# One change to a linear-attention and MLP kernel: the MLP's second product by Strassen's method

## The chip, the cores and the metric

The kernel runs on one core of one Trainium2 chip. A core has a matrix engine (TensorE, "PE" in the profile, with its weight loads listed as "PEld"), three engines for elementwise work (VectorE "DVE", ScalarE "ACT", GpSimd "POOL"), and a synchronising engine ("SP") that issues nearly all DMA transfers of this kernel. The metric is the device time of one execution in microseconds (us); lower is better. Several executions are timed, and the median is what counts.

## The reference

Two layers with the same weights, on an input x of 2048 tokens by D = 448. Each layer is a linear-attention block and then an MLP block, both with a layer norm in front and a residual add behind:

```
def _A_ref(x, wqkv, wo):          # 16 heads of 28
    q, k, v = split(x @ wqkv)
    pq, pk = phi(q), phi(k)       # phi(t) = (t + 1 if t > 0 else exp(t)) + 1e-6
    kv = einsum("bhsd,bhse->bhde", pk, v);  z = sum of pk over s
    o = (pq @ kv) / (pq . z + 1e-6)
    return o @ wo

def _B_ref(x, w1, b1, w2, b2):    # F = 1792
    h = gelu(x @ w1 + b1)         # tanh approximation
    return h @ w2 + b2

x = x + _A_ref(layernorm(x), ...)
x = x + _B_ref(layernorm(x), ...)     # and both once more
```

All inputs and outputs are float32. The change touches only `h @ w2`: per layer a 2048 x 1792 matrix times a 1792 x 448 matrix.

## The kernel before, in words

**Arithmetic.** Matmuls use a one-pass type, `float32r`, which keeps fewer bits than float32. To get the accuracy back, each float32 operand is split into a high part (a cast to float32r) and a low part (the operand minus its high part), and each product is made of three matmuls: high x high, high x low, low x high. All three accumulate into the same PSUM bank. The masked key-value product (L681) and the transposes are plain float32 and have no split.

**Attention.** Tokens are handled in 16 tiles of 128. A tile is loaded (`ld`), normalised (`a`, `ar`, `n`), transposed through VectorE's 32 x 32 transposes and a trip to DRAM (`tu`, `st`, `sp`; early tiles by TensorE), and split (`xh`, `xl`) into the buffers XH and XL. TensorE then makes keys and queries (`K`, `Q`, helper `proj`, L547 to L552) and accumulates a Gram matrix in four PSUM banks (`G`). After the last tile the key-value matrix is formed (`kv`, L681), masked to its heads and folded with `wo`. In a second pass over the tiles the queries come back from DRAM (`pl`), are divided by their denominators (`pz`, `pd`, `pm`), transposed (`pu`, `ps`, `pp`, `qh`, `ql`) and multiplied with the folded matrix (`o`, `oc`); `oa` adds the residual, and `la`, `ln`, `mu`, `ms`, `mp`, `yh`, `yl` make the normalised, transposed and split input of the MLP. `lb` adds b2 to x ahead of time.

**MLP.** Tokens go in 4 blocks of 512 per layer. For each block and each of NF = 14 chunks of 128 hidden units, `f` makes the first product transposed (hidden units on partitions, 512 tokens along the free axis; 11 matmuls of 512 columns, L891 to L895), `g` applies bias and Gelu on ScalarE, `gh` casts the high part on ScalarE, `gl` subtracts on VectorE, and `y` adds this chunk's share to the second product: for each of the block's 4 token tiles three matmuls of 448 columns (L918 to L920), with the activation as the stationary operand and w2's parts as the moving one. The four sums stay in the four PSUM banks "acc" for the whole block; `ya` adds them to x, and `ys` stores the tile.

The second product's core is

```
pe.matmul(o, gh[:, r], w2h[:, i, s], start=first, stop=False)
pe.matmul(o, gh[:, r], w2l[:, i, s], start=False, stop=False)
pe.matmul(o, gl[:, r], w2h[:, i, s], start=False, stop=last)
```

**Memory and order.** w1 and w2 are staged piece by piece in layer 0 (`bld`, `bhi`, `blo`; pieces 16 to 29 are w2) and stay in SBUF as high and low parts. Intermediate tiles live in rings with a fixed number of buffers (`BUFS`); the next user of a buffer waits until all readers of its last content are done. The MLP's input for a block takes one of two XH/XL buffers. PSUM has eight banks: four "acc", two "h", two "m". The order of all instructions is written out by hand in `ORDER`, one list of tokens per layer; a token is an operation's name, its tile or chunk number, and after a colon an engine or buffer choice (`a`, `d`, `p`: ScalarE, VectorE, GpSimd). A token with ">" belongs to the next layer, one with "<" to the layer before. Each engine, and SP's DMA queue, runs its own instructions strictly in this order, and waits where an operand is not ready; an instruction behind a waiting one waits too.

## Time and profile before

| | us |
|---|---|
| median of 3 runs | 877.58 |
| lowest and highest run | 875.4 and 878.11 |
| profiled execution: span, first to last instruction (the page gives no other time of it) | 875.6 |
| TensorE busy in it | 870.3 |
| VectorE, ScalarE, GpSimd busy | 477.5, 344.2, 208.7 |
| moved by DMA | 93.71 MB |

A row of a group reads: line, engine, operation, tile written <- tiles read, shapes, count, then total busy time and the mean of one in nanoseconds, then how long the engine was idle just before, and what ended that. A row of the timeline reads: start, duration, engine, line, operation, count. Matmuls overlap in the records, so the distance between the starts of two of them is what one costs, not its duration.

### The profile page before, as it was taken

The numbers are of one execution on the slowest core, as the hardware profiler recorded it, in microseconds if no ns is written. First come the engines' busy times: TensorE is split into PE (matmuls) and PEld (weight loads), VectorE is DVE, ScalarE is ACT, GpSimd is POOL, SyncE is SP. The second block draws the span as 40 slices with busy tenths as digits, with TensorE's granted clock in tenths as the row PEclk, the third lists the DMA queues.
The fourth block names the chain that finished last, engine by engine and source line by source line (L and its number), as shares of the span: only waits on it lengthen the run. The fifth ranks groups of instructions, "written<-read, shape, count | busy, mean of one in ns | idle before, by whom it ended". The sixth has DMA issues, their size and how long they took to land.

```text
span 875.6 us, 11616 instructions
## 1 busy us (share of the span) xinstructions
PE 870.3 (99%) x4189; PEld 774.1 (88%) x4189; DVE 477.5 (55%) x974; ACT 344.2 (39%) x610; POOL 208.7 (24%) x247
## 2 busy tenths in 40 slices
PE   9999999999999999999999999999999999999998
PEld 7999998889888888888899999889898888888887
DVE  7887687758543534442379756875735616212112
ACT  6676744323223223322446555341332232223222
POOL 4555552543210020020022325240311110200000
PEclk9999999999999999999999999999999999999999
DMA  7666545543314203220347442363341251021101
GB/s 240 188 179 223 132 137 160 169 149 94 111 57 107 84 17 112 81 75 25 82 149 232 155 117 64 101 203 109 118 107 43 73 130 64 1 73 36 42 1 43
DMA packets 62762, 93.71 MB, mean 107 GB/s; under 512 B 8816, under 2 KB 57968, under 8 KB 62704
## 3 DMA queue, kind: packets, MB, share of 16 engines
q1 hardware_dynamic: 62400, 92.51, 35.1%
q8 instruction: 33, 0.54, 0.3%
q10 hardware_dynamic: 304, 0.46, 0.2%
q14 instruction: 25, 0.20, 0.1%
HBM read 55.65 MB, written 34.08 MB: 102 GB/s over the span
## 4 chain that ended last, share of the span: by engine, by line
PE 90%; issue 3%; DVE 2%; DMA 2%; ACT 1%; POOL 1%; SPq 0%; POOLq 0%; DVEq 0%; ACTq 0%
PE y L919 10%; PE y L918 10%; PE y L920 10%; PE hp L892 9%; PE hp L891 9%; PE hp L893 9%; PE hp L894 3%; PE hp L895 3%; PE psq L547 2%; PE psq L548 2%; PE psq L549 2%; PE op L827 2%; PE op L828 2%; PE op L826 2%; PE psk L547 1%
## 5 line engine op out<-in xcount | busy, mean ns | idle before, releaser
L910 DVE TENSOR_TENSOR gl<-g,gh 128x512 fp32r<-128x512 f32 x112 | 81.3, 729 | 265.1 <-ACT gh L215 265.1
L900 ACT ACTIVATE g<-hp,b1s 128x512 f32<-128x512 f32 x112 | 76.9, 688 | 258.1 <-PE hp L895 236.1
L919 PE MATMUL y<-w2l,gh 128*128 128x448 f32 x448 | 163.7, 365 | 0.0
L918 PE MATMUL y<-w2h,gh 128*128 128x448 f32 x448 | 163.6, 365 | 0.0
L920 PE MATMUL y<-w2h,gl 128*128 128x448 f32 x448 | 163.6, 365 | 0.0
L892 PE MATMUL hp<-XH,w1l 128*128 128x512 f32 x336 | 130.9, 390 | 0.0
L891 PE MATMUL hp<-XH,w1h 128*128 128x512 f32 x336 | 130.8, 389 | 0.0
L893 PE MATMUL hp<-XL,w1h 128*128 128x512 f32 x336 | 130.8, 389 | 0.0
L215 ACT CAST gh<-g 128x512 fp32r<-128x512 f32 x112 | 69.2, 621 | 137.8 <-PE y L919 131.7
L361 POOL TENSOR_TENSOR brs<-bve,mhalf 128x1 f32<-128x1 f32 x64 | 37.3, 586 | 358.7 <-DVE bve L355 325.5
L918 PEld LDWEIGHTS y<-w2h,gh 128*128 128x128 f32 x448 | 84.1, 188 | 7.4
L919 PEld LDWEIGHTS y<-w2l,gh 128*128 128x128 f32 x448 | 84.1, 188 | 7.3
L920 PEld LDWEIGHTS y<-w2h,gl 128*128 128x128 f32 x448 | 84.1, 188 | 6.6
L893 PEld LDWEIGHTS hp<-XL,w1h 128*128 128x128 f32 x336 | 63.1, 188 | 13.2
L891 PEld LDWEIGHTS hp<-XH,w1h 128*128 128x128 f32 x336 | 63.1, 188 | 12.6
L892 PEld LDWEIGHTS hp<-XH,w1l 128*128 128x128 f32 x336 | 63.1, 188 | 12.5
L757 POOL TENSOR_TENSOR pz<-pq,zb 128x448 f32<-128x448 f32 x32 | 37.3, 1170 | 50.0 <-DVE dn L762 37.1
L539 POOL TENSOR_TENSOR xnl<-x,xnh 128x384 fp32r<-128x384 f32 x32 | 32.6, 1017 | 58.4 <-ACT xnh L215 58.3
L351 DVE BATCH_NORM_STATS2 bst<-x 128x6 f32<-128x448 f32 x64 | 39.5, 617 | 7.7 <-DMA x<-in_A_x_dram 4.2
L894 PE MATMUL hp<-XH,w1x 128*128 128x512 f32 x112 | 43.6, 389 | 0.0
L895 PE MATMUL hp<-XL,w1x 128*128 128x512 f32 x112 | 43.6, 389 | 0.0
L855 POOL TENSOR_TENSOR x<-x,b2b 128x448 f32<-128x448 f32 x32 | 39.5, 1246 | 14.9 <-DVE xm L365 14.9
(174 smaller groups left out, 1569.2 us busy)
## 6 DMA issues: line engine op xcount, KB each, us to landing
x<-in_A_x_dram SPq DMA_DIRECT2D x32, 224.0 KB, 3.5
pq_d<-eq SPq DMA_DIRECT2D x32, 224.0 KB, 2.9
pq<-pq_d SPq DMA_DIRECT2D x32, 224.0 KB, 3.4
x<-x_d SPq DMA_DIRECT2D x32, 224.0 KB, 3.3
sq_a<-sq SPq DMA_DIRECT2D x13, 512.0 KB, 3.0
sp<-sq_a SPq DMA_DIRECT2D x52, 128.0 KB, 3.5
sq_q<-sq SPq DMA_DIRECT2D x12, 512.0 KB, 3.6
sp<-sq_q SPq DMA_DIRECT2D x48, 128.0 KB, 3.1
```

Of the source, the lines that this page charges most:

```text
L215: act.copy(out, src)
L351: dve.bn_stats(st, xs)
L891: pe.matmul(o, w1h[:, c, s], x.moving(x.hi, c), start=(c == 0), stop=False)
L892: pe.matmul(o, w1l[:, c, s], x.moving(x.hi, c), start=False, stop=False)
L893: pe.matmul(o, w1h[:, c, s], x.moving(x.lo, c), start=False, stop=False)
L894: pe.matmul(o, w1x[:, s], x.moving(x.hi, 3), start=False, stop=False)
L895: pe.matmul(o, w1x[:, s], x.moving(x.lo, 3), start=False, stop=True)
L900: act.activation(T[l, "g", n], T[l, "hp", n], AF.Gelu_apprx_tanh, bias=b1s[:, n % NF:n % NF + 1])
L910: dve.tensor_sub(lo, T[l, "g", n], f(hi))
L918: pe.matmul(o, gh[:, r], w2h[:, i, s], start=first, stop=False)
L919: pe.matmul(o, gh[:, r], w2l[:, i, s], start=False, stop=False)
L920: pe.matmul(o, gl[:, r], w2h[:, i, s], start=False, stop=last)
```

## The change

w2 is no longer kept in SBUF. Per block of 512 tokens, the Gelu output is seen as a 2 x 2 matrix of quadrants: token halves of 256 by hidden halves of KC = 7 chunks. w2 is a 2 x 2 matrix too: hidden halves by column halves of HD = 224. Strassen's method in Winograd's form makes the 2 x 2 product from seven products of quadrants or sums of them (P1 to P7), instead of eight.

- **Weights, once, in layer 0** (`vd`, `va`, `vh`, `vl`, `vs`): for each of 7 pairs of chunks both rows of w2 are loaded, the seven weight operands (w2's quadrants and three sums) are made, split into high and low parts, and stored in a DRAM tensor `w2_d`.
- **Reloads** (`cw`): each product of each block reads its 128 x 3136 floats (high and low side by side) from `w2_d` into one of three buffers "Y": 7 x 4 x 2 = 56 reloads, on SP's queue.
- **Activations**: `g` now writes a whole block's Gelu output into a store (the second XH and XL buffers and a new tile `g6`); the MLP's input keeps one XH/XL buffer per layer. `cs` makes the four activation sums on GpSimd, in place where it can, in four pieces each; `ch` and `cl` split each product's operand (four pieces, in rings A/B or E/F), on ScalarE and VectorE.
- **Products** (`cp`): for each piece, chunk and token tile, one matmul of 448 columns (high activation against high and low weights side by side) and one of 224 columns (low activation against high weights, into the right half of the bank). Each product uses two "acc" banks.
- **Results**: `ca` (ScalarE) and `cf` (VectorE) take the two halves of a bank out of PSUM, into a temporary tile or straight onto x; `cx` (GpSimd) adds the temporaries to x's quadrants.
- Gone are `gh`, `gl`, `y`, `u`, `ya` and the w2 pieces of `bld`, `bhi`, `blo`. Everything else does the same work, and both lists of `ORDER` are rewritten throughout.

The diff, with the lists cut to a few lines:

```diff
--- before.py
+++ after.py
 ORDER = (
     (
-        "ld0 a0 ar0 ld1 a1 n0 hot16 wkld0 wkld1:a wkld2 wkld3:a wkh1 wkl1 ht0 wkh0 ar1 wkl0 n1 d0 ht1 hx0 hl0 "
...
+        "ld0 hot16 fl a0 ar0 ld1 a1 ar1 wkld0 wkld1:a tab0 tab1 >tab0 n0 ht0 n1 wkld2 wqld0 wkld3 wqld1 ld3 wkh0 "
...
+        "cs61 ca48 cl102 cs62 >ar4 cs63 cf48 cl104 cp102 ch105:aEF cl105 >st1 cw26 cp103 cf50 "
...
     ),
 )
@@ -140,6 +169,8 @@
     G = 112
     NG = D // G
     TL = D - 64
+    HD = D // 2
+    KC = NF // 2
     LAYERS = 2
 
     consts = ctx.enter_context(tc.tile_pool(name="consts", bufs=1))
@@ -149,7 +180,7 @@
     psum = ctx.enter_context(tc.tile_pool(name="psum", bufs=1, space=bass.MemoryType.PSUM))
     ctx.enter_context(tc.manual_schedule())
 
-    BUFS = {"H": 9, "S": 5, "e": 3, "xn": 2, "A": 2, "B": 2, "E": 2, "F": 2, "X": 2, "tail": 2, "small": 2}
+    BUFS = {"H": 9, "S": 5, "e": 3, "xn": 2, "A": 2, "B": 2, "E": 2, "F": 2, "X": 2, "tail": 2, "small": 2, "Y": 3}
     BANKS = {"acc": 4, "h": 2, "m": 2}
 
     def dram(shape, dt, name):
@@ -168,6 +199,7 @@
         return smalls.tile([128, n], F32, name=name, tag=name, bufs=BUFS["small"])
 
     pq_d = [dram([S, D], F32, f"pq_d{l}") for l in range(LAYERS)]
+    w2_d = dram([7, 128, KC * D], F32, "w2_d")
     x_d = [x0] + [dram([S, D], F32, f"x_d{l}") for l in range(1, LAYERS)] + [y_out]
 
     ones = consts.tile([128, 128], F32R, name="ones")
@@ -195,8 +227,7 @@
     w1h = wts.tile([128, 3, F], F32R, name="w1h")
     w1l = wts.tile([128, 3, F], F32R, name="w1l")
     w1x = wts.tile([128, F], F32R, name="w1x")
-    w2h = wts.tile([128, NF, D], F32R, name="w2h")
-    w2l = wts.tile([128, NF, D], F32R, name="w2l")
+    g6 = wts.tile([128, 6, 512], F32, name="g6")
 
     def rows(t):
         return slice(t * 128, (t + 1) * 128)
@@ -311,18 +342,12 @@
     def bld(l, n, e):
         tag = e or "xn"
         s = T[l, "bg", n] = ring(tag, 512 if tag == "xn" else D, "stg")[:, :D]
-        if n < 16:
-            load_piece(w1[:, n // 4 * D:(n // 4 + 1) * D], n % 4, s, sp)
-        else:
-            sp.dma_start(s, w2[rows(n - 16), :])
+        load_piece(w1[:, n // 4 * D:(n // 4 + 1) * D], n % 4, s, sp)
 
     @op
     def bhi(l, n, e):
         s = T[l, "bg", n]
         eng = ENG[e or "a"]
-        if n >= 16:
-            copy(eng, w2h[:, n - 16], s)
-            return
         sl, c = slice(n // 4 * D, (n // 4 + 1) * D), n % 4
         if c < 3:
             copy(eng, w1h[:, c, sl], s)
@@ -335,14 +360,48 @@
     def blo(l, n, e):
         s = T[l, "bg", n]
         eng = ENG[e or "p"]
-        if n >= 16:
-            eng.tensor_tensor(w2l[:, n - 16], s, f(w2h[:, n - 16]), op=OP.subtract)
-            return
         sl, c = slice(n // 4 * D, (n // 4 + 1) * D), n % 4
         if c < 3:
             eng.tensor_tensor(w1l[:, c, sl], s, f(w1h[:, c, sl]), op=OP.subtract)
         else:
             eng.tensor_tensor(w1x[64:128, sl], s[64:128], f(T[l, "bt", n][64:128]), op=OP.subtract)
+
+    P1, P7, P6, P5, P2, P3, P4 = range(7)
+
+    @op
+    def vd(l, i, e):
+        T["w2o", l, i] = o = ring("Y", KC * D, "w2o").rearrange("p (k h n) -> p k h n", k=7, h=2)
+        sp.dma_start(o[:, P1:P5 + 1:P5 - P1, 1], w2[rows(i), :].rearrange("p (h n) -> p h n", h=2))
+        sp.dma_start(o[:, P2:P3 + 1, 1], w2[rows(KC + i), :].rearrange("p (h n) -> p h n", h=2))
+
+    @op
+    def va(l, i, e):
+        o = T["w2o", l, i][:, :, 1]
+        eng = ENG[e or "p"]
+        eng.tensor_tensor(o[:, P7], o[:, P3], o[:, P5], op=OP.subtract)
+        eng.tensor_tensor(o[:, P5], o[:, P5], o[:, P1], op=OP.subtract)
+        eng.tensor_tensor(o[:, P6], o[:, P3], o[:, P5], op=OP.subtract)
+        eng.tensor_tensor(o[:, P4], o[:, P2], o[:, P6], op=OP.subtract)
+
+    @op
+    def vh(l, i, e):
+        hi, lo = (T["w2o", l, i][:, :, h] for h in range(2))
+        copy(ENG[e or "a"], hi.bitcast(F32R), lo)
+
+    @op
+    def vl(l, i, e):
+        hi, lo = (T["w2o", l, i][:, :, h] for h in range(2))
+        (ENG[e or "p"]).tensor_tensor(lo.bitcast(F32R), lo, hi, op=OP.subtract)
+
+    @op
+    def vs(l, i, e):
+        sp.dma_start(w2_d[:, :, i * D:(i + 1) * D].rearrange("k p n -> p k n"),
+                     T["w2o", l, i].rearrange("p k h n -> p k (h n)"))
 
@@ -365,9 +424,9 @@
         dve.tensor_scalar(out, xs, mv[:, 0:1], rs, op0=OP.subtract, op1=OP.mult)
 
     class Block:
-        def __init__(self):
-            self.hi = ring("XH", 2048, "XH", F32R)
-            self.lo = ring("XL", 2048, "XL", F32R)
+        def __init__(self, r):
+            self.hi = ring(f"XH{r}", 2048, "XH", F32R)
+            self.lo = ring(f"XL{r}", 2048, "XL", F32R)
 
         def pieces(self, t):
             s = slice(t * 512, (t + 1) * 512)
@@ -379,11 +438,10 @@
         def still(self, x, t, c):
             return x[:, (t * 4 + c) * 128:(t * 4 + c + 1) * 128]
 
-    BUFS["XH"] = BUFS["XL"] = 2
-
-    def block(*key):
+    def block(kind, l, b):
+        key = (kind, l, b) if kind == "a" else (kind, l)
         if ("blk", key) not in T:
-            T["blk", key] = Block()
+            T["blk", key] = Block(b % 2)
         return T["blk", key]
 
@@ -894,47 +952,124 @@
         pe.matmul(o, w1x[:, s], x.moving(x.hi, 3), start=False, stop=False)
         pe.matmul(o, w1x[:, s], x.moving(x.lo, 3), start=False, stop=True)
 
+    def gstore(l):
+        if (l, "G2") not in T:
+            T[l, "G2"] = [ring(t, 2048, "g2").rearrange("p (c n) -> p c n", c=4) for t in ("XH1", "XL1")]
+        return T[l, "G2"]
+
+    def gview(l, half, c, k=1):
+        return gstore(l)[half][:, c:c + k] if c < 4 else g6[:, half * 3 + c - 4:half * 3 + c - 4 + k]
+
     @op
     def g(l, n, e):
-        T[l, "g", n] = ring("e", 512, "g")
-        act.activation(T[l, "g", n], T[l, "hp", n], AF.Gelu_apprx_tanh, bias=b1s[:, n % NF:n % NF + 1])
-
-    @op
-    def gh(l, n, e):
-        T[l, "gs", n] = ring("A", 512, "gh", F32R), ring("B", 512, "gl", F32R)
-        copy(ENG[e or "a"], T[l, "gs", n][0], T[l, "g", n])
-
-    @op
-    def gl(l, n, e):
-        hi, lo = T[l, "gs", n]
-        dve.tensor_sub(lo, T[l, "g", n], f(hi))
-
-    def y_mm(l, n, j, s=slice(0, D), o=None):
-        gh, gl = T[l, "gs", n]
         i = n % NF
-        first, last = i == 0, i == NF - 1
-        r = rows(j)
-        o = T[l, "y", n // NF, j][:, s] if o is None else o
-        pe.matmul(o, gh[:, r], w2h[:, i, s], start=first, stop=False)
-        pe.matmul(o, gh[:, r], w2l[:, i, s], start=False, stop=False)
-        pe.matmul(o, gl[:, r], w2h[:, i, s], start=False, stop=last)
-
-    @op
-    def y(l, n, e):
-        for j in range(4):
-            u(l, n * 4 + j, e)
-
-    @op
-    def u(l, n, e):
-        n, j = divmod(n, 4)
-        if n % NF == 0:
-            T[l, "y", n // NF, j] = bank("acc", f"y{j}")[:, :D]
-        y_mm(l, n, j)
-
-    @op
-    def ya(l, t, e):
-        xs = T["x", l, t]
-        dve.tensor_tensor(xs, T[l, "y", t // 4, t % 4], xs, op=OP.add)
+        act.activation(gview(l, i // KC, i % KC)[:, 0], T[l, "hp", n], AF.Gelu_apprx_tanh, bias=b1s[:, i:i + 1])
+
+    def quad(l, r, c, q):
+        return gview(l, c, q * 2, min(2, KC - q * 2))[:, :, r * 256:(r + 1) * 256]
+
+    def sums(l, n):
+
+        bk, q = divmod(n, 4)
+        k = bk % 7
+        if k == P7:
+            return T[l, "s3", bk // 7 * 4 + q]
+        return quad(l, *{P1: (0, 0), P6: (0, 0), P5: (1, 0), P2: (0, 1), P3: (0, 1), P4: (1, 1)}[k], q)
+
+    @op
+    def cs(l, n, e):
+        (b, s), q = divmod(n // 4, 4), n % 4
+        a11, a12, a21, a22 = quad(l, 0, 0, q), quad(l, 0, 1, q), quad(l, 1, 0, q), quad(l, 1, 1, q)
+        eng = ENG[e or "p"]
+        if s == 0:
+            w = a11.shape[1]
+            T[l, "s3", b * 4 + q] = ring("e", 512, "s3")[:, :w * 256].rearrange("p (c n) -> p c n", c=w)
+        out, x, y, o = ((T[l, "s3", b * 4 + q] if s == 0 else None, a11, a21, OP.subtract),
+                        (a21, a21, a22, OP.add), (a11, a21, a11, OP.subtract), (a12, a12, a11, OP.subtract))[s]
+        eng.tensor_tensor(out, x, y, op=o)
+
+    @op
+    def ch(l, n, e):
+        x = sums(l, n)
+        w = x.shape[1]
+        T[l, "chl", n] = [ring(t, 512, nm, F32R)[:, :w * 256].rearrange("p (c n) -> p c n", c=w)
+                          for t, nm in zip(e[1:] or "AB", ("ch", "cl"))]
+        copy(ENG[e[:1] or "a"], T[l, "chl", n][0], x)
+
+    @op
+    def cl(l, n, e):
+        hi, lo = T[l, "chl", n]
+        ENG[e or "d"].tensor_tensor(lo, sums(l, n), f(hi), op=OP.subtract)
+
+    @op
+    def cw(l, n, e):
+        T[l, "w2", n] = ring("Y", KC * D, "w2s", F32R).rearrange("p (c n) -> p c n", c=KC)
+        ENG[e or "s"].dma_start(f(T[l, "w2", n].rearrange("p c n -> p (c n)")), w2_d[n % 7])
+
+    @op
+    def cp(l, n, e):
+        bk, q = divmod(n, 4)
+        hi, lo = T[l, "chl", n]
+        w = T[l, "w2", bk]
+        if q == 0:
+            T[l, "cp", bk] = [bank("acc", f"cp{j}")[:, :D] for j in range(2)]
+        for c in range(hi.shape[1]):
+            i = q * 2 + c
+            for j in range(2):
+                o = T[l, "cp", bk][j]
+                pe.matmul(o, hi[:, c, rows(j)], w[:, i], start=(i == 0), stop=False)
+                pe.matmul(o[:, HD:], lo[:, c, rows(j)], w[:, i, :HD], start=False, stop=(i == KC - 1))
+
+    @op
+    def ca(l, n, e):
+        bk, j = divmod(n, 2)
+        key = (l, "ctt", bk)
+        if key not in T:
+            tag = "e" if bk // 7 == 3 else "W6" if bk % 7 == P7 else "W5"
+            T[key] = ring(tag, 512 if tag == "e" else D, "ct")[:, :D]
+        T[l, "ct", n] = T[key][:, j * HD:(j + 1) * HD]
+        copy(ENG[e or "a"], T[l, "ct", n], T[l, "cp", bk][j][:, :HD])
+
+    @op
+    def cf(l, n, e):
+
+        bk, j = divmod(n, 2)
+        b, k = divmod(bk, 7)
+        o = T[l, "cp", bk][j]
+        if k in (P2, P3, P4):
+            r, c = {P2: (0, 0), P3: (0, 1), P4: (1, 0)}[k]
+            xs = T["x", l, 4 * b + 2 * r + j][:, c * HD:(c + 1) * HD]
+            dve.tensor_tensor(xs, o[:, :HD], xs, op=OP.add)
+            dve.tensor_tensor(xs, o[:, HD:], xs, op=OP.add)
+            return
+        if k == P6:
+            t = T[l, "ct", n] = T[l, "ct", (b * 7 + P1) * 2 + j]
+            dve.tensor_tensor(t, o[:, :HD], t, op=OP.add)
+        t = T[l, "ct", n]
+        dve.tensor_tensor(t, o[:, HD:], t, op=OP.add)
+
+    @op
+    def cx(l, n, e):
+
+        (bk, j), eng = divmod(n, 2), ENG[e or "p"]
+        b, k = divmod(bk, 7)
+        t = T[l, "ct", n]
+
+        def add(r, c, v):
+            xs = T["x", l, 4 * b + 2 * r + j][:, c * HD:(c + 1) * HD]
+            eng.tensor_tensor(xs, xs, v, op=OP.add)
+
+        if k == P1:
+            add(0, 0, t)
+        elif k == P6:
+            s = T[l, "ct", (b * 7 + P7) * 2 + j]
+            eng.tensor_tensor(s, s, t, op=OP.add)
+            add(0, 1, t)
+            add(1, 0, s)
+            add(1, 1, s)
+        else:
+            add(0, 1, t)
+            add(1, 1, t)
 
     @op
     def ys(l, t, e):
```

More of the change, by code (lines that the diff above doesn't have):

```diff
@@ L902, in gh @@
-    @op
-    def gh(l, n, e):
-        T[l, "gs", n] = ring("A", 512, "gh", F32R), ring("B", 512, "gl", F32R)
-        copy(ENG[e or "a"], T[l, "gs", n][0], T[l, "g", n])
-    @op
-    def gl(l, n, e):
-        hi, lo = T[l, "gs", n]
-        dve.tensor_sub(lo, T[l, "g", n], f(hi))
-    def y_mm(l, n, j, s=slice(0, D), o=None):
-        gh, gl = T[l, "gs", n]
-        i = n % NF
-        first, last = i == 0, i == NF - 1
-        r = rows(j)
-        o = T[l, "y", n // NF, j][:, s] if o is None else o
-        pe.matmul(o, gh[:, r], w2h[:, i, s], start=first, stop=False)
-        pe.matmul(o, gh[:, r], w2l[:, i, s], start=False, stop=False)
-        pe.matmul(o, gl[:, r], w2h[:, i, s], start=False, stop=last)
@@ L922, in y @@
-    @op
-    def y(l, n, e):
-        for j in range(4):
-            u(l, n * 4 + j, e)
-    @op
-    def u(l, n, e):
-        n, j = divmod(n, 4)
-        if n % NF == 0:
-            T[l, "y", n // NF, j] = bank("acc", f"y{j}")[:, :D]
-        y_mm(l, n, j)
-    @op
-    def ya(l, t, e):
-        xs = T["x", l, t]
-        dve.tensor_tensor(xs, T[l, "y", t // 4, t % 4], xs, op=OP.add)
+        i = n % NF
+        act.activation(gview(l, i // KC, i % KC)[:, 0], T[l, "hp", n], AF.Gelu_apprx_tanh, bias=b1s[:, i:i + 1])
```

215 rows, old and new, of the table ORDER are left out of this document.

## The prediction

> **What bounds the kernel now.** I read the page first: busy times, then the chain of waits.
>
> ```profile
> span 875.6 us, 11616 instructions
> PE 870.3 (99%) x4189; PEld 774.1 (88%) x4189; DVE 477.5 (55%) x974; ACT 344.2 (39%) x610; POOL 208.7 (24%) x247
> ...
> q1 hardware_dynamic: 62400, 92.51, 35.1%
> ...
> PE 90%; issue 3%; DVE 2%; DMA 2%; ACT 1%; POOL 1%; SPq 0%; POOLq 0%; DVEq 0%; ACTq 0%
> ```
>
> TensorE is busy from end to end (at full granted clock, 1.00 in the stage rows below) and carries 90% of the chain that sets the end; every other engine is at 55% or less. So time is won only by giving TensorE less work, and lost wherever it must wait. What it works on is in the costliest groups:
>
> ```profile
> L919 PE MATMUL y<-w2l,gh 128*128 128x448 f32 x448 | 163.7, 365 | 0.0
> L918 PE MATMUL y<-w2h,gh 128*128 128x448 f32 x448 | 163.6, 365 | 0.0
> L920 PE MATMUL y<-w2h,gl 128*128 128x448 f32 x448 | 163.6, 365 | 0.0
> ...
> L918 PEld LDWEIGHTS y<-w2h,gh 128*128 128x128 f32 x448 | 84.1, 188 | 7.4
> ```
>
> The 365 ns are not a price: matmuls overlap in these records. The price is the distance between starts, so I read TensorE's timeline in the MLP of the first layer: 20 matmuls of the second product in a row, then the same line of the first product two groups later.
>
> ```profile
> 399.69 0.36 PE L919 MATMUL y<-w2l,gh 128*128 128x448 f32 x1
> ...
> 403.54 0.36 PE L920 MATMUL y<-w2h,gl 128*128 128x448 f32 x1
> ...
> 406.26 0.39 PE L891 MATMUL hp<-XH,w1h 128*128 128x512 f32 x1
> ...
> 411.25 0.39 PE L891 MATMUL hp<-XH,w1h 128*128 128x512 f32 x1
> ```
>
> A 448-column matmul costs 3.85 us / 19 = 202.6 ns; a 512-column one 4.99 / 22 = 226.8 ns. The second product is now 3 x 448 = 1344 matmuls of 448 columns: 272.3 us, 31% of the span. Only this part shrinks.
>
> **What TensorE does instead.** Per 512 tokens there are 7 products; each has 7 chunks x 2 token tiles, and for each of these one matmul of 448 columns (high part of the activation against both parts of the weight) and one of 224 (low part against the high part only). With 8 groups of 512 tokens that is 784 pairs: 784 x 202.6 ns = 158.8 us for the wide ones, and 784 narrow ones whose price x decides all. Break-even is x = (272.3 - 158.8) / 784 = 144.7 ns.
>
> No row shows a one-pass matmul of 224 columns. The nearest: the line through the two prices above has a slope of 24.2 ns / 64 columns = 0.378 ns, and gives 202.6 - 224 x 0.378 = 118 ns. But each matmul brings its own weight load, and a narrow one may not hide it. Loads under short matmuls are seen in the masked key-value product, 112 columns each:
>
> ```profile
> 109.75 3.33 PEld L681 LDWEIGHTS kvp<-gt,wvt 128*112 128x112 f32 x32
> 109.95 3.31 PE L681 MATMUL kvp<-gt,wvt 128*112 128x112 f32 x32
> 113.03 0.45 PE L547 MATMUL psq<-wq,XH 128*128 128x448 f32 x1
> ...
> 113.00 0.19 PEld L547 LDWEIGHTS psq<-wq,XH 128*128 128x128 f32 x1
> 113.11 0.19 PEld L548 LDWEIGHTS psq<-wq,XH 128*128 128x128 f32 x1
> ```
>
> 32 loads and matmuls run from 109.95 to 113.03: 96.3 ns each, although one load's record is about 180 ns. So loads are pipelined; scaled from 112 to 128 weights that is 110 ns, and the two loads that follow (128 weights, this kernel's one-pass type) also start 110 ns apart. A load therefore allows 110 ns and the line asks 118; I take 114, between. The ends for the range are two rows that would hold if this reading is wrong: 202.6 ns, the closest that one-pass matmuls ever follow each other in the long runs, and 2 x 96.3 x 224 / 112 = 385 ns, if a narrow matmul ran as the plain f32 product of L681 does (16 products of 112 columns per layer appear as 32 records). A pure 224 x 0.378 = 85 ns I exclude below: it lies under every distance of two such loads.
>
> At 114 ns: 784 x (202.6 + 114) = 248.2 us, **24.1 us less** than 272.3; at 110, 27.2 less; at 118, 21.0 less.
>
> The Trainium skill speaks against the narrow half: "TensorE: Matmul & The Clock Gate", section "LDWEIGHTS (loading the stationary operand)", puts a load at columns / 1.2 ns, an estimate of 107 ns for 128, longer than 224 columns take to stream; the narrow matmul would be bound by its load. With 107 ns the sum would be 30 us less, without the overhead that the rows show.
>
> **What the other engines get.** Prices from rows grouped by shape:
>
> ```profile
> L910 DVE TENSOR_TENSOR gl<-g,gh 128x512 fp32r<-128x512 f32 x112 | 81.3, 729 | 265.1 <-ACT gh L215 265.1
> ...
> L481 DVE TENSOR_TENSOR XL<-tp,XH 128x256 fp32r<-128x256 f32 x4 | 1.6, 421 | 1.0 <-ACT XH L215 1.0
> ...
> L215 ACT CAST gh<-g 128x512 fp32r<-128x512 f32 x112 | 69.2, 621 | 137.8 <-PE y L919 131.7
> ...
> L539 POOL TENSOR_TENSOR xnl<-x,xnh 128x384 fp32r<-128x384 f32 x32 | 32.6, 1017 | 58.4 <-ACT xnh L215 58.3
> ...
> L540 POOL TENSOR_TENSOR xnh<-x,xnh 128x64 fp32r<-128x64 f32 x32 | 12.0, 376 | 0.0
> ```
>
> Per 512 tokens. ScalarE: 14 casts of 512 go (8.7 us); 21 of 512 and 7 of 256, at no more than 0.621 each, come (17.4), with 6 half-width copies out of PSUM (under 3.7). VectorE: 14 subtractions of 512 and 4 adds of 448 go (12.8; the line through the 512 and 256 rows gives 0.65 for 448); 21 of 512 and 7 of 256 (18.3) and 22 adds of 224 columns (0.38 each by the same line, 8.4) come, 26.7. GpSimd: 2.0 ns a column by its two rows, so 12 sums of 512 at 1.27, 4 of 256 at 0.76 and 14 half-width adds at 0.70: 28.1 us new. This all lies beside TensorE's 14 first-product groups (154 x 226.8 = 34.9 us) and 98 pairs (31.0): 66.0 us a block, before 68.9. How full is that cover? The busy time by stage:
>
> ```profile
> 170.00:230.00 60.00, 60.00 (x283) 52.87 (x282) 37.54 (x75) 19.53 (x35) 18.32 (x16) 1.00 0.37 112
> 230.00:300.00 70.00, 70.00 (x333) 62.21 (x332) 34.20 (x66) 18.43 (x30) 7.72 (x8) 1.00 0.28 80
> ```
>
> (columns: TensorE, loads, VectorE, ScalarE, GpSimd busy, clock, share of the DMA engines, GB/s). Scaled to a block of 68.9 us, VectorE has 43.1 in the first stage: minus 12.8, plus 26.7: 57 of 66. GpSimd: 21.0 + 28.1 = 49 of 66. In the second stage VectorE comes to 48. So the extra work is hidden, most tightly in the first block of layer 0, where VectorE is 87% full; past that each microsecond is TensorE's. The preparation of the weight sums (14 stagings go, 7 come, their low parts on VectorE) lies in layer 0's attention, where the page's first slices have VectorE at 7 to 8 tenths; I cost it at nothing, and some 20 us of VectorE work lands there.
>
> **The reloads.** 56 reloads of 128 x 3136 x 4 bytes, 1.606 MB each, on SP's queue, into 3 slots; 90 MB beside today's 93.7. The queue row gives 92.51 MB in 35.1% of 875.6 us: 301 GB/s while the engines are busy.
>
> ```profile
> sq_a<-sq SPq DMA_DIRECT2D x13, 512.0 KB, 3.0
> ```
>
> From the 512 KB row, 1568 KB take 3.0 + 1.08 MB / 301 GB/s = 6.6 us at best and 3.06 x 3.0 = 9.2 at worst. A reload can start when the product three earlier is done. At the tightest, at the end of layer 1, only two products lie between, 2 x 14 x 316.6 ns = 8.9 us; where first-product groups lie between, each adds 2.5 us, and pricing the new list along TensorE leaves 10.8 or more nearly everywhere. So 6.6 is hidden; at 9.2 three reloads are late by 0.3 each, 0.9 us, and I charge that. Behind a waiting reload stand, on SP, the loads and stores that carry the next block's transposes; each may be up to 5.3 us (1.606 MB / 301) later than now.
>
> **Start and end.** At the start the list puts table changes before the first weight cast, and that cast now comes second:
>
> ```profile
> 2.44 1.28 ACT L215 ACT_TABLE_LOAD   x1 [2.44 <-issue]
> ...
> 6.97 0.57 ACT L215 CAST wk<-stg 128x448 fp32r<-128x448 f32 x1 [2.05 <-DMA stg<-in_A_wqkv_dram]
> ```
>
> The load fits into the 2.05 us that ScalarE waits there for a DMA; one cast of 0.57 moves behind it: +0.6. At the end four adds and a store follow the last matmul now, four half-width adds and a store later: nothing.
>
> **Sum:** -24.1 + 0.9 + 0.6 = -22.6. On the profiled execution's span of 875.6 that is 853.0; the median of the runs is 2.0 above that span (877.58), so 855.0.
>
> **Rivals.**
> *The narrow matmul is not cheap* (slower). Place: the 784 narrow matmuls. If the load's 188 ns were time that it holds the array, x is 202.6: 784 x 405.2 = 317.7, +45.4, 923 us; if it runs as L681 does, x = 385, 460.7, +188.4, 1066 us. It decides from 144.7 ns on. For it: no one-pass matmul in the long runs follows another in under 202.6 ns, and none under 448 columns exists in this trace. Against it: L681's loads, recorded as long, every 96 ns. The Trainium skill's "Perfetto Trace Analysis", section "Identifying the Most-Contended Engine", judges TensorE's headroom by load busy time. By the rows that is 88% here, and 224 more loads of 188 ns would make it (4189 + 224) x 188 = 830 us of 855; taken as a bound it would eat all the gain. Chance 0.12.
>
> *Half the gain is lost to waits.* First-product inputs are now one buffer per layer instead of two: the next block's inputs are written only after the last first-product group of this block, and they come through SP's queue behind reloads. Six such hand-overs, 2 us each, and the 87% VectorE stage: 12 us, 867 us. For it: the DMA share rises from 0.28 to about 0.85 in that stage (7 x 5.3 = 37 of 66 us added). Against it: the list leaves second-product work between. Chance 0.15.
>
> *The same waits at full price:* six hand-overs each late by the 5.3 us of a reload ahead, 32 us, 887 us. Chance 0.07.
>
> **How the numbers follow.** Forecast 855 (0.66; its own range 850 to 861: x from 110 to 118, waits from 0 to 5 us). To leave out no more than 2 in 10, I reach from 848 to 885: outside lie the narrow-matmul rival (0.12), about half of the full-price one and a little below. A measurement of this kernel tells about 0.3% (2.6 us) from no change. Faster: forecast and most of the half-lost case, 0.78; same 0.05, from the edges of both wait cases; slower 0.17.
>
> **What would show it.** In the changed profile: starts of wide and narrow second-product matmuls alternate at 203 and 114 ns; were the narrow distance over 145, the forecast falls whatever else happens. TensorE's idle time before the second product's groups should name no DMA of the weight sums for more than 1 us in all, and the reloads should land in 6 to 9 us. VectorE should rise to some 610 us (477.5 + 8 x 13.9 + 20), ScalarE to 443 at most (344.2 + 8 x 12.4), GpSimd to about 430 (208.7 + 8 x 28.1). A gap of several microseconds at the start of a block's first product would show the hand-over; gaps inside the products that end with VectorE would show that its cover is gone.

## The result, and the profile after

The changed kernel takes 914.98 us (median of 4 runs, 912.85 to 917.23) against 877.37 beside it: a ratio of 1.043, 95% interval 1.0409 to 1.0451. It is 4.3% slower; the forecast of 855 and its range up to 885 are both missed, and the change goes the other way.

The page of the changed kernel: span, busy times, the main DMA queue, the chain of waits by engine, the costliest groups of the second product, and the reloads.

```profile
span 912.8 us, 13007 instructions
PE 867.5 (95%) x4413; PEld 757.9 (83%) x4413; DVE 675.9 (74%) x1253; ACT 414.3 (45%) x767; POOL 475.9 (52%) x485
...
q1 hardware_dynamic: 78800, 193.89, 64.3%
...
PE 54%; DVE 20%; POOL 10%; issue 8%; ACT 3%; DMA 2%; SPq 0%; DVEq 0%; POOLq 0%; ACTq 0%
...
L1020 PE MATMUL cp<-w2s,ch 128*128 128x448 f32 x784 | 255.5, 376 | 1.7 <-DVE ct L1049 1.2
L1002 DVE TENSOR_TENSOR cl<-g,ch 128x512 fp32r<-128x512 f32 (+1 forms) x192 | 161.7, 863 | 98.7 <-ACT ch L246 87.3
L1021 PE MATMUL cp<-w2s,cl 128*128 128x224 f32 x784 | 213.6, 272 | 22.1 <-DVE cl L1002 21.7
...
w2s<-w_d SPq DMA_DIRECT2D x56, 1568.0 KB, 7.3
```

Before, TensorE carried 90% of the chain; now it carries 54%, and VectorE and GpSimd 30% between them. So the kernel is no longer bound by TensorE all the way, although TensorE is still listed as 95% busy (its records overlap and fill small gaps).

Did TensorE's work shrink? The timeline of a run of pairs without waits:

```profile
214.04 0.37 PE L1020 MATMUL cp<-w2s,ch 128*128 128x448 f32 x1
214.25 0.26 PE L1021 MATMUL cp<-w2s,cl 128*128 128x224 f32 x1
214.35 0.38 PE L1020 MATMUL cp<-w2s,ch 128*128 128x448 f32 x1
...
216.86 0.38 PE L1020 MATMUL cp<-w2s,ch 128*128 128x448 f32 x1
```

From 214.04 to 216.86 are 9 pairs: 313 ns each (predicted 316.6). 784 pairs cost 245.6 us instead of 272.3: **26.7 us less**, as hoped. With nothing else changed the span would be 875.6 - 26.7 = 848.9. It is 912.8, so 63.9 us of new loss have to be found. The waits of TensorE, by what ended them:

```profile
PE cp L1021 <- DVE cl L1002: 21.7, 30, 1.9
PE hp L951 <- DVE XL L490: 6.8, 5, 2.3
```

and who is behind it on the other engines:

```profile
ACT ch L246 <- PE cp L1020: 143.7, 85, 5.5
...
ACT ch L246 <- POOL g L989: 36.9, 23, 6.9
PEld cp L1021 <- DVE cl L1002: 34.6, 44, 2.1
```

TensorE waits for VectorE's low parts: of the second product (`cl`) and of the first product's input (`XL`). No wait of TensorE names a reload, and these land in 7.3 us, inside the 6.6 to 9.2 of the prediction. The listed idle time is less than 63.9. One reason is that the record of the matmul ahead of a wait lasts longer (0.38 us at 214.35) than the distance to the next start (0.21 at 214.04) and covers the beginning of the wait.

The stretches of the first block of layer 0, in windows of 10 us (columns as in the prediction):

```profile
180.00:190.00 10.00, 9.53 (x50) 8.15 (x49) 7.88 (x12) 4.57 (x10) 6.41 (x6) 1.00 0.92 279
...
212.00:222.00 10.00, 6.90 (x40) 5.64 (x38) 9.93 (x11) 4.50 (x9) 8.86 (x8) 1.00 0.90 322
222.00:232.00 10.00, 9.93 (x45) 8.25 (x46) 8.73 (x21) 2.46 (x4) 3.53 (x4) 1.00 0.69 266
```

Where TensorE is at 6.90 of 10, VectorE is at 9.93 and GpSimd at 8.86. But look at the counts: VectorE is full with 11 instructions in 10 us, and nearly as full with 21. Its instructions have become longer. By shape (VectorE's and GpSimd's groups):

```profile
L1002 DVE TENSOR_TENSOR cl<-g,ch 128x512 fp32r<-128x512 f32 x144 | 130.1, 918 | 71.3 <-ACT ch L246 60.1 <-PE cp L1021 10.8
L490 DVE TENSOR_TENSOR XL<-sp,XH 128x512 fp32r<-128x512 f32 x50 | 49.6, 1007 | 4.1 <-ACT XH L246 2.0 <-DMA x<-x_d 2.0
...
L1049 DVE TENSOR_TENSOR ct<-cp,ct 128x224 f32<-128x224 f32 x64 | 23.9, 381 | 9.6 <-ACT ct L246 9.0
```

The subtraction `cl` of 512 columns takes 918 ns, where the same operation (`gl`) took 729 before, and XL 1007 where it took 749. The add of 224 columns that reads PSUM (L1049) takes 381 ns, the 0.38 of the prediction. What do the long ones have in common? The timeline of three places, both engines together (the last also with TensorE):

```profile
358.92 1.31 POOL L989 TENSOR_TENSOR g<-g,g 128x512 f32<-128x512 f32 x1 [0.62 <-ACT g L966]
359.38 1.40 DVE L1002 TENSOR_TENSOR cl<-s,ch 128x512 fp32r<-128x512 f32 x1 [0.68 <-ACT ch L246]
...
739.26 1.93 POOL L1060 TENSOR_TENSOR x<-x,ct 128x224 f32<-128x224 f32 x2
739.51 3.30 DVE L490 TENSOR_TENSOR XL<-sp,XH 128x512 fp32r<-128x512 f32 x3
740.85 0.40 PE L950 MATMUL hp<-XH,w1l 128*128 128x512 f32 x1
742.86 0.50 PE L951 MATMUL hp<-XL,w1h 128*128 128x512 f32 x1 [1.61 <-DVE XL L490]
...
886.47 0.68 DVE L1002 TENSOR_TENSOR cl<-g,ch 128x512 fp32r<-128x512 f32 x1
887.95 0.67 POOL L1066 TENSOR_TENSOR ct<-ct 128x224 f32<-128x224 f32 x1 [1.99 <-DVE ct L1049]
...
891.57 3.44 POOL L989 TENSOR_TENSOR g<-g,g 128x512 f32<-128x512 f32 x2
892.24 0.39 DVE L1049 TENSOR_TENSOR ct<-cp,ct 128x224 f32<-128x224 f32 x1
```

Alone, a `cl` of 512 takes 0.68 (886.47) and a GpSimd add of 224 takes 0.67 (887.95). At 359.38 a `cl` starts while a GpSimd sum runs that began at 358.92 and ends at 360.23. The `cl` ends at 360.78, 0.55 us after the sum: it does its work only once GpSimd's instruction is over. At 739.51 three XL take 3.30 us instead of 3 x 0.68 = 2.04, beside GpSimd adds, and TensorE loses 1.61 us waiting for them. At 892.24 an add that reads PSUM runs inside a GpSimd sum in 0.39 us, undisturbed. So the reading is: **an elementwise instruction of VectorE with both inputs in SBUF, and a GpSimd instruction on SBUF, exclude each other for the whole length of one instruction.**

The whole trace bears this out. Of the 168 `cl` of 512 columns, the 61 that meet no GpSimd instruction take 645 to 694 ns; the 107 that meet one take up to 1777. In 68 cases a GpSimd sum or add is running when the `cl` starts; in 67 of them the `cl` ends 0.545 to 0.578 us after that instruction, whether it has 224, 256 or 512 columns, and in the last one 0.547 us after the add that follows directly. GpSimd pays as well: an add of 224 takes 0.665 us (median) where it meets no `cl` or XL, and 1.11 where it starts during one. "Both inputs in SBUF" is not the whole rule: the normalising TENSOR_SCALAR of L424, which reads one tile and two values per row, takes 423 to 514 ns where it meets no GpSimd instruction and up to 1481 where it does. The transposes of L460 do not change (567 and 569 ns).

The Trainium skill's "SBUF — State Buffer", section "SBUF: two separate sides", says that the two engines share a port pair that is locked for a whole instruction; the 0.55 us after the sum's end agree. The prediction had not weighed it.

### The profile page after: what moved, and what is told of

The parts are those of the page before. It is cut to its first block, busy times and chain, and to the rows that moved or that the text cites. A ratio compares the mean times of both kernels' runs of the same rounds, so it can differ in the third digit from the quotient of the medians.

```text
span 912.8 us, 13007 instructions
## 1 busy us (share of the span) xinstructions
PE 867.5 (95%) x4413; PEld 757.9 (83%) x4413; DVE 675.9 (74%) x1253; ACT 414.3 (45%) x767; POOL 475.9 (52%) x485
## 4 chain that ended last, share of the span: by engine, by line
PE 54%; DVE 20%; POOL 10%; issue 8%; ACT 3%; DMA 2%; SPq 0%; DVEq 0%; POOLq 0%; ACTq 0%
PE cp L1020 9%; DVE cl L1002 6%; PE hp L951 6%; PE hp L949 6%; PE hp L950 6%; PE cp L1021 5%; POOL g L989 3%; DVE XL L490 2%; PE hp L952 2%; PE hp L953 2%; POOL x L1060 2%; DVE pq L828 1%; PE op L886 1%; PE psq L605 1%; PE psq L606 1%
## 5 line engine op out<-in xcount | busy, mean ns | idle before, releaser
L1020 PE MATMUL cp<-w2s,ch 128*128 128x448 f32 x784 | 255.5, 376 | 1.7 <-DVE ct L1049 1.2
L1002 DVE TENSOR_TENSOR cl<-g,ch 128x512 fp32r<-128x512 f32 (+1 forms) x192 | 161.7, 863 | 98.7 <-ACT ch L246 87.3
L1021 PE MATMUL cp<-w2s,cl 128*128 128x224 f32 x784 | 213.6, 272 | 22.1 <-DVE cl L1002 21.7
L246 ACT CAST ch<-g 128x512 fp32r<-128x512 f32 (+1 forms) x192 | 106.5, 566 | 168.6 <-PE cp L1020 116.0
L1021 PEld LDWEIGHTS cp<-w2s,cl 128*128 128x128 f32 x784 | 150.4, 192 | 38.0 <-DVE cl L1002 34.6
L1020 PEld LDWEIGHTS cp<-w2s,ch 128*128 128x128 f32 x784 | 148.2, 189 | 15.0 <-issue 1.5
L1060 POOL TENSOR_TENSOR x<-x,ct 128x224 f32<-128x224 f32 x96 | 84.0, 898 | 41.2 <-DVE ct L1049 41.2
L989 POOL TENSOR_TENSOR g<-g 128x512 f32<-128x512 f32 (+1 forms) x64 | 78.4, 1230 | 21.9 <-ACT g L966 18.7
L989 POOL TENSOR_TENSOR g<-g,g 128x512 f32<-128x512 f32 x32 | 45.4, 1424 | 30.7 <-ACT g L966 27.8
L490 DVE TENSOR_TENSOR XL<-sp,XH 128x512 fp32r<-128x512 f32 x50 | 49.6, 1007 | 4.1 <-ACT XH L246 2.0
```

What stands on the lines that cost most here:

```text
L246: act.copy(out, src)
L490: dve.tensor_sub(squares(lo), spread_tile(kind, l, t), f(squares(hi)))
L989: eng.tensor_tensor(out, x, y, op=o)
L1002: ENG[e or "d"].tensor_tensor(lo, sums(l, n), f(hi), op=OP.subtract)
L1020: pe.matmul(o, hi[:, c, rows(j)], w[:, i], start=(i == 0), stop=False)
L1021: pe.matmul(o[:, HD:], lo[:, c, rows(j)], w[:, i, :HD], start=False, stop=(i == KC - 1))
```

## The experiments

The theory (A, later A1) is this exclusion. Against it stand: VectorE simply having too much work (B); the reloads, by their traffic or by coming late (C); GpSimd's results merely coming late (A2); and too few buffers between ScalarE, VectorE and TensorE (D). Each run is compared with the kernel before on the same chip, and with the changed kernel's 914.98.

**Sums out of the way.** All of GpSimd's new sums and adds touch one column, and the product P7 reads a plain quadrant instead of its sum, so their real work is left out.

```
-        eng.tensor_tensor(out, x, y, op=o)                   # cs
+        out, x, y = (v[:, :1, :1] for v in (out, x, y))
+        eng.tensor_tensor(out, x, y, op=o)
-            eng.tensor_tensor(xs, xs, v, op=OP.add)          # cx, and s likewise
+            eng.tensor_tensor(xs[:, :1], xs[:, :1], v[:, :1], op=OP.add)
```

> Changes: every GpSimd sum of activations and every GpSimd add of a temporary onto x works on 1 column instead of 224 to 512 (the rest of these sums is left out, and the P7 product reads the plain quadrant); instructions, waits, TensorE work and reloads stay. Theory A (VectorE instructions with two SBUF operands stand still while a GpSimd instruction runs): the 512-column subtraction of the low part falls from 918 ns mean to about 700, VectorE from 676 us by about 60 to 90, and TensorE's waits from 72 us to under 25, so 855 to 870 us. Theory B (VectorE is simply too full, contention is minor): the subtraction stays above 850 ns and the time above 900 us. Theory C (reloads on SP's queue delay the inputs): time above 895 us, the wait of the first product on its input stays.

872.23 us, ratio 0.994 (0.992 to 0.996): 42.7 us of the 63.9 go away with the sums. That is 2 us above the range that A gave; B and C (above 900 and 895) are out as the whole story. VectorE's busy time falls from 675.9 to 603.8 us although not one of its instructions was removed; the prediction's figure for it was 610. That shows what the sums cost, not yet how.

**Reloads cut to a seventh.** Only the first of seven chunks is loaded, and all matmuls of a product use it.

```
-        ENG[e or "s"].dma_start(f(T[l, "w2", n].rearrange("p c n -> p (c n)")), w2_d[n % 7])
+        ENG[e or "s"].dma_start(f(T[l, "w2", n][:, 0]), w2_d[n % 7][:, :D])
```

> Changes: each reload brings only the first of 7 chunks and all matmuls of a product use that chunk (wrong weights, same matmuls, same waits); reload traffic falls from 90 to 13 MB. Theory A: nothing much, 908 to 915 us. Theory B: the same. Theory C: the time falls by more than 20 us, to under 893, and the first product's wait on its input goes.

915.63 us, 1.0435 (1.0414 to 1.0456): the same as the changed kernel, with 13 MB of reloads instead of 90. The reloads and their traffic cost nothing that can be measured.

**The new work on VectorE.** If the two engines only disturb each other, the short VectorE form of the same sums should do better. First the adds `cx` alone, then sums and adds.

```
-        (bk, j), eng = divmod(n, 2), ENG[e or "p"]           # cx
+        (bk, j), eng = divmod(n, 2), dve
-        eng = ENG[e or "p"]                                  # cs, in the second kernel only
+        eng = dve
```

> Changes: only the adds of temporaries onto x (112 half-width adds) move from GpSimd to VectorE; result unchanged. Theory A: VectorE gets 40 us and loses part of its standing still, GpSimd falls by 100 us to 375; time 895 to 912 us. Theory B: VectorE to 716 us or more, time above 920 us. Theory C: close to 915 us.

> Changes: the activation sums and the adds of temporaries onto x move from GpSimd to VectorE, in the same places of the list; result unchanged. GpSimd falls by about 250 us to 215. Theory A: VectorE gets 15 us of work a block (120 us in all) but loses its standing still (about 100 us), so it stays near 690 to 720 us; the 512-column subtraction falls to about 720 ns; time between 875 and 905 us. Theory B: VectorE goes to 790 us, time above 930 us. Theory C: no statement but a time close to 915 us.

925.92 us (1.0557, 1.0539 to 1.0574) and 925.73 (1.0553, 1.0536 to 1.0569): some 11 us slower than the changed kernel, where a gain was expected. Both expectations are missed in their times, although VectorE's busy time in the second (710.6 us) came out as A gave it. The groups, waits and 10 us windows of the second kernel show why:

```profile
L1002 DVE TENSOR_TENSOR cl<-g,ch 128x512 fp32r<-128x512 f32 x144 | 104.1, 735 | 56.1 <-ACT ch L246 46.9 <-PE cp L1021 8.6
...
PE cp L1021 <- DVE cl L1002: 30.1, 30, 2.3
...
190.00:200.00 10.00, 8.47 (x46) 7.49 (x45) 9.79 (x19) 3.94 (x8) 1.59 (x3) 1.00 0.56 189
...
210.00:220.00 10.00, 7.20 (x42) 6.02 (x42) 9.86 (x23) 3.67 (x8) 1.15 (x1) 1.00 0.85 271
```

`cl` is down to 735 ns, so the exclusion is mostly gone; but VectorE stands at 9.8 of 10 all the same, now with 19 and 23 instructions in 10 us, and TensorE waits longer for `cl`. In the products VectorE has no room for this work: per block TensorE needs 98 x 0.313 = 30.7 us for them, and VectorE 21 x 0.68 + 7 x 0.42 = 17.2 for `cl` and 22 x 0.38 = 8.4 for adds out of PSUM; the sums (12 x 0.68 + 4 x 0.42 = 9.8) and the adds (14 x 0.38 = 5.3) make it 40.7. So by this sum there are two limits, not one: shared with GpSimd the exclusion, alone the work itself. The instructions also kept the places that the list had given them for GpSimd, so on VectorE they now stand in line ahead of some `cl`; a list laid out anew was not run, and how much of the 11 us is due to that stays open.

**Is it the exclusion or the lateness?** On top of the one-column kernel, GpSimd is kept busy again: by powers of one column, which touch next to nothing of SBUF, or by adds of 128 x 128; two behind each sum, one behind each add.

```
+    def filler(n):
+        for _ in range(n):
+            pool.tensor_tensor(scrap[:, :1], tiny, mhalf, op=OP.pow)    # first kernel
+            pool.tensor_tensor(scrap, ident, f(ones), op=OP.add)        # second kernel
```

> Changes: the 1-column sums of run e1, and behind each of them GpSimd work of about the old length (two powers of one column, 0.55 us each, behind a sum of activations; one behind an add onto x) that moves almost no data. GpSimd is as busy and as late as in the changed kernel, but hardly touches SBUF. Theory A1 (what costs is that GpSimd and VectorE exclude each other on SBUF): 512-column subtraction 690 to 780 ns, time 868 to 885 us, near e1's 872. Theory A2 (what costs is that GpSimd is late with the sums, and the splits wait for it): 905 to 920 us, with the subtraction below 780 ns.

> Changes: as e5, but the GpSimd work behind each 1-column sum adds two 128 x 128 SBUF tiles into a third (about 0.5 us each) that no other instruction uses. GpSimd is about as busy, and now it reads and writes SBUF. Theory A1: the 512-column subtraction rises to 850 to 950 ns although nothing waits for these adds, time 895 to 920 us, at least 20 us above e5. Theory A2: like e5.

885.07 us (1.0096, 1.0067 to 1.0125) and 883.57 (1.0079, 1.005 to 1.0108). Both add 11 to 13 us to 872.23. The powers show what lateness alone costs, 12.8 us: ScalarE's `ch` waits for the sums almost as long as in the changed kernel (32.0 against 36.9 us), while `cl` is not held up. The adds miss what A1 gave them (895 to 920 us) and come out as A2 said, like the powers. `cl` in the first and the second kernel:

```profile
L1008 DVE TENSOR_TENSOR cl<-g,ch 128x512 fp32r<-128x512 f32 x168 | 122.8, 743 | 100.7 <-ACT ch L246 84.4 <-PE cp L1027 15.4
...
L1008 DVE TENSOR_TENSOR cl<-g,ch 128x512 fp32r<-128x512 f32 x168 | 131.1, 793 | 91.0 <-ACT ch L246 73.7 <-PE cp L1027 12.5 <-PE hp L953 3.9
```

The exclusion is there beside the adds too: of the 70 `cl` that start during one of them, 57 end 0.54 to 0.58 us after it. But an add of 128 columns takes only 0.46 us (median), VectorE's busy time rises by no more than 23 us (598.0 to 621.0), and TensorE's wait for `cl` hardly moves (5.8 to 7.3 us). So this much of it stays hidden. What instructions of the real length do is seen in the pair with the same shapes, below.

**More buffers.** The rings of `ch` and `cl` get 5 buffers instead of 2. To make room, reloads are cut as above and only the first piece of the weight sums is prepared; the second kernel has the same cuts and 2 buffers.

```
-    BUFS = {... "A": 2, "B": 2, ...}
+    BUFS = {... "A": 5, "B": 5, "YW": 3, ... "Y": 1}       # second kernel: "A": 2, "B": 2
```

> Changes: the rings that hold the split operands of a product (A and B) have 5 buffers instead of 2; to make room the reloads bring one chunk of seven and the weight sums are prepared for the first pair of chunks only (wrong weights, same matmuls; preparation in layer 0's attention mostly left out). Theory D (the splits of one piece cannot start until the piece two before has been multiplied, so the chain cast, subtract, multiply is too short of buffers): ScalarE's 144 us of waiting for a product falls by more than half and the time falls to 870 to 890 us. Theory A1 alone: within 8 us of e8, since VectorE stands still as before.

> Changes: the control of e7, with the same short reloads and left-out preparation, and 2 buffers as in the changed kernel. All theories: 905 to 916 us, a few us under the changed kernel, from layer 0's attention alone.

905.68 us (1.0331, 1.0301 to 1.0361) and 911.15 (1.0394, 1.0344 to 1.0443): 5.5 us from three more buffers, and with two runs each the intervals still overlap. The wait of ScalarE's `ch` for TensorE falls from 155.7 us in the second kernel to 17.4, and yet nearly all of the loss stays, above the 870 to 890 us that D gave. D is at most a small part.

**The same shapes, results unused.** From the one-column kernel with the cuts of the last pair (second kernel here, the control), the first kernel adds behind each one-column sum or add a GpSimd add of the width that the sum had (512, 256 or 224 columns), on a scratch tile that nobody reads.

```
+    def filler(n):
+        pool.tensor_tensor(scrap[:, 1, :n], scrap[:, 0, :n], scrap[:, 2, :n], op=OP.add)
```

> Changes: e8's base (short reloads, two split buffers), with e1's 1-column sums, and behind each 1-column sum one GpSimd add of the old width (512 or 256 columns behind a sum, 224 behind an add onto x) on a scratch tile that nothing else reads. GpSimd's instructions thus have the length and SBUF traffic of the changed kernel, but nothing waits for their results. Theory A1, now with the length of an instruction in it (a VectorE instruction with two SBUF operands waits for the end of the GpSimd instruction that runs, so a 1.29 us one costs more than two of 0.46): 512-column subtraction 880 to 930 ns, time 895 to 912 us, at least 20 above e12. Theory A2 (lateness of the sums): within 15 us of e12, subtraction below 800 ns.

> Changes: e8's base with e1's 1-column sums and adds, no filler: the control of e9. All theories: 866 to 872 us, e1's 872 less the few us of layer 0's preparation.

915.79 us (1.0436, 1.0415 to 1.0457) against 868.72 (0.9899, 0.988 to 0.9919): **47.1 us** from GpSimd work whose results go nowhere, about as much as the real sums cost (42.7). That is far more than A2 allowed (15) and 4 us above the range that A1 gave. The page and groups of the first:

```profile
PE 869.0 (95%) x4413; PEld 760.6 (83%) x4413; DVE 637.4 (70%) x1231; ACT 405.2 (44%) x761; POOL 511.1 (56%) x718
...
L1018 DVE TENSOR_TENSOR cl<-g,ch 128x512 fp32r<-128x512 f32 x168 | 144.4, 872 | 87.3 <-ACT ch L247 76.0 <-PE cp L1037 10.6
...
PE cp L1037 <- DVE cl L1018: 21.5, 24, 2.6
```

and the same of the control:

```profile
PE 852.4 (98%) x4413; PEld 757.7 (87%) x4413; DVE 585.5 (68%) x1231; ACT 404.4 (47%) x761; POOL 264.2 (30%) x477
...
L1013 DVE TENSOR_TENSOR cl<-g,ch 128x512 fp32r<-128x512 f32 x168 | 122.5, 741 | 104.0 <-ACT ch L246 87.3 <-PE cp L1032 15.4 <-issue 0.4
...
PE cp L1032 <- DVE cl L1013: 3.0, 5, 0.9
```

The same 1231 instructions of VectorE take 637.4 us instead of 585.5, `cl` 872 ns instead of 741, and TensorE's wait for `cl` goes from 3.0 to 21.5 us. GpSimd is as busy as with the powers (511 against 486 us), but the powers cost 12.8 us and these adds 47.1. So, as an estimate by difference between kernels with different cuts, some 13 us may be put down to lateness (the one-column sums queue behind the filler here too) and the other 34 to exclusion by long instructions.

**Shorter sums.** Each `cs` is cut into two instructions of half the columns, or four of a quarter.

```
-        eng.tensor_tensor(out, x, y, op=o)
+        for h in range(2):                                   # second kernel: 4
+            r = slice(h * 256 // 2, (h + 1) * 256 // 2)
+            eng.tensor_tensor(out[:, :, r], x[:, :, r], y[:, :, r], op=o)
```

> Changes: each activation sum on GpSimd is two instructions of half the columns; result unchanged. Theory A1 with length: VectorE waits for shorter instructions, the 512-column subtraction falls from 918 to about 850 ns, GpSimd rises by about 30 us, time 900 to 912 us. Theory A2: GpSimd is later, time 915 to 930 us.

> Changes: as e10 with four instructions of a quarter each. GpSimd rises by about 90 us over the changed kernel. Theory A1 with length: subtraction about 800 ns, but GpSimd later; 895 to 920 us. Theory A2: above 930 us.

913.25 us (1.0412, 1.0395 to 1.0429), not told apart from the changed kernel and between the two forecasts, and 930.2 (1.06, 1.0584 to 1.0616), 15 us slower: there A1's 895 to 920 is missed, and the time is the one that A2 gave (above 930). Page and waits of the kernel with four:

```profile
PE 879.2 (95%) x4413; PEld 766.1 (83%) x4413; DVE 636.6 (69%) x1253; ACT 412.9 (44%) x767; POOL 550.4 (59%) x869
...
ACT ch L246 <- POOL g L991: 75.4, 35, 5.9
...
PE cp L1022 <- ACT ch L246: 12.9, 13, 2.1
```

VectorE gets back 39 us (675.9 to 636.6), in the direction that the exclusion calls for. But GpSimd pays 74 more (475.9 to 550.4), its sums come later, the casts wait for them twice as long (75.4 against 36.9 us), and TensorE now waits 12.9 us for `ch`, while its wait for `cl` stays nearly what it was (19.2 against 21.7). No kernel that keeps all the work came out faster than the one before.

## Why the prediction was wrong

- **The narrow matmul**, the term on which it said all depends: right. A pair takes 313 ns against 316.6, and if the wide one still takes 202.6, the narrow one takes 111, in its range of 110 to 118. The term is -26.7 instead of -24.1. The slower rival, that the narrow matmul is not cheap, is out: the kernel is slower for another reason.
- **The reloads:** landing in 7.3 us, in the range; the 0.9 us charged for lateness were not needed. The rivals that send the loss through SP's queue at the block's hand-over are not what happened either: TensorE's waits for XL end with VectorE, not with a DMA, and a seventh of the reload bytes changes nothing. Their prices, 867 and 887 us, were both too low. One of them did name the stage in which VectorE is 87% full, but not GpSimd beside it.
- **"So the extra work is hidden"** is the step that failed: it was priced at nothing, and 42.7 us of the 63.9 us of new loss go away when GpSimd's sums and adds are taken out. It went wrong in two ways. It gave VectorE (57 of 66 us) and GpSimd (49 of 66) each the whole block as its own cover, as if they never met; 57 + 49 is 106, and the traces show that much of this cannot run at the same time. And it took the average of a block, while the new work lies in the products: 30.7 us a block, for which VectorE has to make 17.2 us of `cl` and GpSimd its 28.1 of sums and adds, 45.3 us of work that excludes itself. Some of it can be done ahead, beside the first product, but the buffers and the order bound how much. The prediction had named the sign of it, gaps inside the products that end with VectorE, and these are what the waits show.
- **VectorE "some 610 us"**: 603.8 with the sums out of the way, so the instructions were counted and priced rightly; 675.9 with them. The 72 us between go with the sums, and the instructions that meet GpSimd are the ones that grew. GpSimd, put at 430, took 475.9, its adds being held up by VectorE in turn; ScalarE 414.3, under its bound of 443.
- The sign was in the profile before, in rows that the prediction used or could have used. It took the mean of `gl`, 729 ns, as a price. The instructions of that line (minimum, median and maximum):

```profile
L910 DVE TENSOR_TENSOR gl<-g,gh x112: 627/692/1726, 142.0 to 867.7; 128x512 fp32r<-128x512 f32 x112
```

A fixed amount of work whose slowest case takes 2.5 times the median is held up by something. The 103 of them that meet no GpSimd instruction take 695 ns at most. With GpSimd at 24% only 9 of 112 met one; with GpSimd at 52% it is 107 of 168.
- What stays open: 21.2 of the 63.9 us (63.9 - 42.7) are still lost with one-column sums. The weight sums in layer 0's attention, which the prediction cost at nothing, are some 3.6 of them: with all but the first piece left out and the reloads short, the ratio falls by 0.0041 (0.994 to 0.9899, and 1.0435 to 1.0394), and short reloads alone change nothing. VectorE's own fill and the clock (below) may be part of the rest; no run separates them. No run laid out the order of the lists anew, and start and end were not looked at separately.

## What to carry to other kernels

Before work is called hidden on VectorE and GpSimd, add up what both of them do on SBUF in the stage where it falls, not over a block and not engine by engine: in this kernel VectorE's subtractions and normalisations on SBUF and GpSimd's wide instructions were one resource. A group whose maximum is far above its median may already be paying for it. VectorE's adds that read PSUM, its transposes, and GpSimd's powers of one column did not count in that sum here, and cutting GpSimd's instructions into pieces added a wait rather than removing one.

## What the runs showed of the hardware

**Half clock after short gaps.** TensorE's granted clock fell to half in three stretches of the changed kernel, each 3.41 us long, never in the middle of the kernel before. Windows over 3.41 us ahead of two of them and in them, and ahead of and in a stretch that did not fall:

```profile
203.88:207.29 3.41, 1.74 (x10) 1.12 (x8) 3.41 (x4) 1.71 (x4) 3.02 (x3) 1.00 0.59 230
207.29:210.71 3.42, 3.12 (x11) 2.90 (x12) 2.22 (x6) 0.93 (x2) 2.37 (x4) 0.50 0.52 153
302.87:306.28 3.41, 1.06 (x6) 0.88 (x6) 3.41 (x4) 0.93 (x2) 3.41 (x3) 1.00 0.00 0
306.28:309.70 3.42, 3.42 (x11) 2.84 (x10) 1.00 (x3) 0.78 (x2) 3.42 (x5) 0.50 0.49 164
...
739.77:743.18 3.41, 1.80 (x10) 1.29 (x9) 3.41 (x4) 1.22 (x3) 3.41 (x4) 1.00 0.98 364
743.18:746.59 3.41, 3.41 (x20) 2.99 (x18) 1.77 (x2) 0.22 (x1) 3.40 (x4) 1.00 0.94 379
```

After a window in which TensorE was busy for 1.74 of 3.41 us the next one ran at 0.50, after one with 1.80 it did not. In half clock a pair takes longer (timeline):

```profile
208.53 0.60 PE L1020 MATMUL cp<-w2s,ch 128*128 128x448 f32 x1
208.93 0.39 PE L1021 MATMUL cp<-w2s,cl 128*128 128x224 f32 x1
209.12 0.60 PE L1020 MATMUL cp<-w2s,ch 128*128 128x448 f32 x1
```

590 ns instead of 313, so by estimate a stretch costs 3.41 x (1 - 313 / 590) = 1.6 us, and the three some 5 of the 63.9 us. The kernel with sums in four has a mean clock of 0.983 against 0.994, which is at most some 10 us of its 928 and may be much of its 15 us loss. The Trainium skill's "TensorE: Matmul & The Clock Gate", section "Why this matters for your kernels", warns of single gaps of over about 3 us; here no single gap in the window at 203.88 is that long (the waits for `cl` there are 1.31 and less), and short gaps that add up to about half a window were enough. Where the limit lies these runs do not show: in the kernel with five buffers a window with TensorE busy for 1.59 us (424.06 to 427.47) was followed by full clock.

**Exclusion goes by whole instructions, if these read and write many columns.** A `cl` that starts during a GpSimd sum or add ends 0.545 to 0.578 us after it in 67 of 68 cases, and beside adds of 128 columns the same is seen in 57 of 70. Beside powers of one column, which are no shorter than these adds (0.55 against 0.46 us, medians), it is not: the 72 `cl` that start during one have a median of 0.68 us, as if alone. What it costs in time is not in proportion: 368 adds of 128 columns add 11.3 us to the kernel, no more than the powers do (12.8), while 240 adds of 224 to 512 columns add 47.1, all of them on scratch data.
